# A list schedule for attention: score pairs two at a time on four banks, transfers costed by their bytes, the first batch's loads and small product moved

## The chip, the core and the metric

The kernel runs on one core of a Trainium2 chip: TensorE (PE, matrix products into eight PSUM banks), VectorE (DVE), ScalarE (ACT), GpSimd (POOL) and SyncE (SP), whose queue issues nearly all transfers here. The metric is the time on the device in microseconds, from launch to the last result; lower is better.

## The reference

Talking-heads attention over 4 batches, 12 heads, 448 positions and 64 channels, then a mixture of experts and a two-layer MLP over the 1792 tokens. The change touches attention alone:

```python
def _attn_ref(q, k, v, w_pre, w_post) -> np.ndarray:
    scale = 1.0 / np.sqrt(q.shape[-1])
    scores = scale * np.matmul(q, k.transpose(0, 1, 3, 2))
    scores = np.einsum('bhij,hg->bgij', scores, w_pre)
    scores = scores - np.max(scores, axis=-1, keepdims=True)
    attn = np.exp(scores)
    attn = attn / (np.sum(attn, axis=-1, keepdims=True) + 1e-09)
    attn = np.einsum('bhij,hg->bgij', attn, w_post)
    return np.matmul(attn, v).astype(np.float32)
```

`w_pre` and `w_post` mix the 12 heads before and after the softmax.

## The kernel before, in words

A batch's 448 query rows are cut into chunks of 120, 120, 120 and 88 rows, 16 chunks X in all, and each chunk into blocks n of ten (or fewer) rows times 12 heads, 180 blocks in all. The work on one chunk:

- **Scores** `s`: K and Q come in as `kn`, `qn`, two heads at a time, are transposed on TensorE (`tp`) and split into a high part (`KH`, `QH`, ScalarE) and a low part (`KL`, `QL`, VectorE). A score pair (`qk`) is six row-tiled matmuls for two heads, into two banks; ScalarE or VectorE copies each bank into `S` (line 557).
- **Relay** `x`: a transfer on SyncE's queue gathers the rows of a block from `S`, heads and rows together on the partitions. Six buffers.
- **Pre-mix** `m`: a full matmul with `kpre`; then the maximum (VectorE), the exponential `E` (ScalarE), three small steps on VectorE up to `kr`, the post-mix weights scaled by the sums.
- **Post-mix** `pa`: four matmuls per block into one bank, copied to `AT`. Blocks are post-mixed in order.
- **Products** `px` with V (column-tiled), then `pt`, the small logits products `pl`, `plt`, `pq`.

Besides runs a side job in 64 pieces: load `W`, one step on ScalarE, three on VectorE, store to `wi` or `wo`.

Chunk 0 of the first batch is written out by hand: K and Q come as `fk` and `fq` in pieces, GpSimd copies them together (`beside`), TensorE transposes and multiplies pair after pair; `repeat` is the small product `wps` that spreads `w_pre` and `w_post` (loaded through GpSimd's queue); `spin` is idle work, matmuls of a constant into a bank that nobody reads. All after that is put in order by `Plan`, a list scheduler that runs when the program is built. Each piece of work is a generator that yields steps with the engines it may run on and (time that the engine is held, time until the result), the buffers it takes (`take`) and gives back, and events. The scheduler takes the step that can start first, ties by rank, with a penalty for a change of TensorE's tiling (`TURN`, `LOYAL`), and the instructions of every engine, SyncE's too, stand in the order in which it took them. It decides nothing on the chip: there each engine works down its queue and waits where a semaphore tells it to. Tiles of the eight banks come from `Banks`, in the plan the bank that the plan gave. SyncE's transfers share eight semaphores in turn, so that each waits for the landing of the eighth before it.

Of the kernel before, what the change touches and what calls it, by code (L numbers as in the profile page):

```python
# [48 lines left out]
class Banks:  # L49


    def __init__(self, pool, n):
        self.pool, self.given, self.turns = pool, [], itertools.cycle(range(n))

    def tile(self, shape, dt, tag, name):
        i = self.given.pop(0) if self.given else next(self.turns)
        return self.pool.tile(shape, dt, tag=f"{tag}{i}", name=name)


class Plan:  # L60
# [8 lines left out]
    HOP, TURN, STAY, LOYAL, DRIFT = 0.06, 0.19, 0.02, 2.0, 0.0  # L69

    def __init__(self, slots, banks=None, seed=0):
        self.free = {t: [(0.0, i) for i in range(n)] for t, n in slots.items()}
        self.at, self.engine, self.pending, self.held = {}, {}, [], {}
        self.now = self.reached = 0.0
# [30 lines left out]
    def run(self):  # L105
        while self.pending:
# [36 lines left out]
            end = start + lat  # L143
            for a in step.get("give", ()):
                tag, key = (a, id(task)) if isinstance(a, str) else a
                s = self.held[tag, key if tag == "q" else 0].pop(0)
                self.free[tag] = sorted(self.free[tag] + [(end, s)])
# [4 lines left out]
        if self.banks:  # L152
            self.banks.given = []
            self.banks.turns = itertools.cycle([s for t, s in self.free["q"]])
# [19 lines left out]
def attention(ctx, qctx, tc, q, k, v, w_pre, w_post, wg, xs, lg, ident, nb=4, side=None, route=None):  # L174
# [72 lines left out]
    for h0, h1 in ((0, 2), (2, 4), (4, 8), (8, H)):  # L247
# [210 lines left out]
    with tc.manual_schedule(engines=START):  # L458
        spin(9)
        for j in range(H // 2 + 1):  # L460
            if j < H // 2:
# [6 lines left out]
                if j == 1:  # L468
                    repeat()
                if j > 0:  # L470
                    ps = qk(0, j - 1)
                split_k(0, j, pk)
# [30 lines left out]
    def dma(d):  # L503
        return {"SP": (0.8, d)}
# [3 lines left out]
    def block(n):  # L508
        X, be, rs, m, M = geom(n)
        yield dict(run=dma(4.2), take=["x"], on=[("S", X, h) for h in range(H)], ends=[("x", n)])  # L510
# [32 lines left out]
    def score(X, j):  # L543
# [6 lines left out]
        for i in (j, j + 1):  # L550
            yield dict(run=pe(0.61), tiling="row", onward=True, take=[("q", ("s", X, i, h)) for h in range(2)], on=on, ends=[("s", X, i)])
# [7 lines left out]
    def heads(b, j, s_):  # L559

        tag, src, t = (("kn", k, KN), ("qn", q, QN))[s_]
        yield dict(run=dma(4.0), take=[tag])
# [12 lines left out]
    def values(b):  # L575
        for g in range(4):
            yield dict(run=dma(3.5), on=[("av", 4 * b - 1, 0), ("av", 4 * b - 1, 1)] if b else [("x", 3)], ends=[("V", b)] if g == 3 else [])
# [60 lines left out]
    def piece(i, load, square, bits, store):  # L638
        yield dict(run=dma(6.0), take=["W"])
# [6 lines left out]
        yield dict(run=dma(3.5), give=["W", "sq"])  # L646
# [3 lines left out]
    for h in range(H):  # L650
        plan.at["S", 0, h] = 0.0
    for j in range(H // 2):
        plan.at["K", 0, j] = plan.at["Q", 0, j] = 0.0
    plan.add(4, values(0))
    plan.engine.update(ACT=1.0, DVE=1.0, PE=0.5, SP=0.0)
    for n in range(N):
        plan.add(n, block(n))
    for X in range(1, len(chunks)):
        n0, nb0 = first_of[X], CH[chunks[X - 1][1]][2]
        for j in range(H // 2):  # L660
            r = n0 - 4 - 8 * (X % 4 == 3) - (H - 2 - 2 * j) * (nb0 - 5) / H
# [1112 lines left out]
```

## Time and profile before

| | |
|---|---|
| three timed runs | 1328.36, 1329.72 (median), 1333.59 us |
| the profiled execution | 1326.42 us, span 1324.7 us, granted clock 0.998 |
| TensorE busy | 1300.1 us (98%), 8855 matmuls |
| VectorE, ScalarE busy | 1042.6 us (79%), 824.0 us (62%) |
| attention | 0 to some 500 us |
| experts, MLP | some 530 to 843.6 us, 843.6 to 1324.7 us |

A busy TensorE is not one at its peak: matmuls overlap, and their ends are modelled. Idle time is what stands between the end of one group and the start of the next, and the profile names what ended it.

### The profile page before, as it was taken

How to read it: one execution, taken by the hardware profiler on the slowest of the kernel's cores; microseconds unless marked ns; L12 is line 12 of the kernel's file. 1: busy time of each engine (PE TensorE's matmuls, PEld its weight loads, DVE VectorE, ACT ScalarE, POOL GpSimd, SP SyncE). 2: the span in 40 equal slices, each digit the busy share in tenths (PEclk: the TensorE clock that was granted, in tenths of full speed). 3: DMA queues.
4: the chain of work that ended last, by engine and by line, in shares of the span. 5: the costliest groups of instructions: out<-in, count | busy, mean ns of one | idle time of the engine just before them, and what ended most of it. 6: DMA issues, size and time to landing. Idle time of an engine off the chain costs nothing.

```text
span 1324.7 us, 24862 instructions
## 1 busy us (share of the span) xinstructions
PE 1300.1 (98%) x8855; PEld 1083.7 (82%) x8855; DVE 1042.6 (79%) x2410; ACT 824.0 (62%) x1509; POOL 67.8 (5%) x84
## 2 busy tenths in 40 slices
PE   8899999999999998999999999999999999999997
PEld 5677777677777777899999999998888888888886
DVE  7687888788778889899999999897666666666663
ACT  6566666566666657888889888765444444444432
POOL 3000000000000000100010000011000000001001
PEclk9999999999999999999999999999999999999999
DMA  6758757675757547278545772464433343224201
GB/s 162 229 192 228 228 169 223 203 235 172 218 188 220 175 153 247 87 270 319 185 167 190 286 266 93 147 225 168 152 101 115 108 132 109 85 96 142 94 25 48
DMA packets 146368, 227.02 MB, mean 171 GB/s; under 512 B 44800, under 2 KB 108480, under 8 KB 146240
## 3 DMA queue, kind: packets, MB, share of 16 engines
q1 hardware_dynamic: 139904, 200.20, 46.9%
q0 software_dynamic: 3744, 18.09, 4.0%
q10 hardware_dynamic: 2592, 7.08, 1.4%
q8 instruction: 73, 1.20, 0.4%
q14 instruction: 55, 0.45, 0.1%
HBM read 217.87 MB, written 31.85 MB: 189 GB/s over the span
## 4 chain that ended last, share of the span: by engine, by line
PE 59%; DVE 0%; ACT 0%; POOLq 0%; issue 0%
PE op L1466 18%; PE dh L1522 17%; PE yp L1280 11%; PE h L1246 11%; PE ph L1267 1%; PE px L1174 1%; PE dpt L1403 1%; POOLq L1769 0%; ACT dhs L1526 0%; ACT r L1489 0%; PE gspg L1023 0%; DVE r L1486 0%; DVE r L1487 0%; DVE o L1474 0%; PE pc L1059 0%
## 5 line engine op out<-in xcount | busy, mean ns | idle before, releaser
L1086 DVE TENSOR_TENSOR wl<-r,wh 128x768 fp32r<-128x768 f32 (+1 forms) x246 | 249.1, 1061 | 11.2 <-ACT wh L1085 8.3
L1085 ACT CAST wh<-r 128x768 fp32r<-128x768 f32 (+1 forms) x246 | 224.2, 931 | 37.9 <-PE h L1246 31.1
L536 PEld LDWEIGHTS pa<-kr,E 120*112 120x112 f32 (+1 forms) x1440 | 166.5, 177 | 45.6 <-issue 31.4
L536 PE MATMUL pa<-kr,E 120*112 120x120 f32 (+1 forms) x1440 | 180.7, 269 | 0.8 <-DVE kr L530 0.4
L1086 DVE TENSOR_TENSOR wil<-wi,wih 128x768 fp32r<-128x768 f32 x64 | 60.9, 953 | 131.3 <-ACT wih L1085 131.3
L515 PE MATMUL m<-x,kpre 120*120 120x448 f32 x360 | 159.8, 548 | 3.9 <-DMA x<-S 3.8
L522 ACT ACTIVATE E<-m,nm 120x448 f32<-120x448 f32 x180 | 114.5, 636 | 57.9 <-DVE nm L518 31.5
L1085 ACT CAST wih<-wi 128x768 fp32r<-128x768 f32 x64 | 53.9, 844 | 155.0 <-PE dh L1522 154.0
L518 DVE TENSOR_REDUCE nm<-m 120x1 f32<-120x448 f32 x180 | 111.2, 619 | 26.5 <-PE m L515 22.0
L1466 PE MATMUL op<-woh,gl 128*128 128x512 f32 x448 | 116.8, 341 | 0.0
L1466 PE MATMUL op<-woh,gh 128*128 128x512 f32 x448 | 116.0, 339 | 0.0
L1466 PE MATMUL op<-wol,gh 128*128 128x512 f32 x448 | 115.3, 338 | 0.0
L1522 PE MATMUL dh<-dxh,wih 128*128 128x512 f32 (+1 forms) x384 | 111.2, 364 | 0.1
L1522 PE MATMUL dh<-dxl,wih 128*128 128x512 f32 (+1 forms) x384 | 110.7, 363 | 0.0
L1522 PE MATMUL dh<-dxh,wil 128*128 128x512 f32 (+1 forms) x384 | 109.9, 363 | 0.0
L539 ACT COPY AT<-pa 112x480 f32<-112x480 f32 (+1 forms) x111 | 63.1, 568 | 43.8 <-PE pa L536 41.3
L1085 ACT CAST woh<-wo 128x768 fp32r<-128x768 f32 x64 | 53.4, 836 | 55.2 <-PE op L1466 54.6
L347 PEld LDWEIGHTS px<-AT,vn 112*64 112x64 f32 x1536 | 73.7, 137 | 10.2 <-issue 4.6
L1466 PEld LDWEIGHTS op<-woh,gh 128*128 128x128 f32 x448 | 70.7, 189 | 11.1 <-DVE o L1474 0.3
L1522 PEld LDWEIGHTS dh<-dxl,wih 128*128 128x128 f32 x384 | 70.1, 189 | 11.5
L1522 PEld LDWEIGHTS dh<-dxh,wil 128*128 128x128 f32 x384 | 69.8, 189 | 11.3
L515 PEld LDWEIGHTS m<-x,kpre 120*120 120x120 f32 x360 | 55.1, 183 | 28.9 <-issue 18.2
(290 smaller groups left out, 2561.1 us busy)
## 6 DMA issues: line engine op xcount, KB each, us to landing
r<-in_moe_w_dram SPq DMA_DIRECT2D x54, 1024.0 KB
r<-in_moe_w_dram SPq DMA_DIRECT2D x72, 768.0 KB
x<-S SPq DMA_DIRECT2D x172, 210.0 KB
wi<-wi SPq DMA_DIRECT2D x32, 768.0 KB
wo<-wo SPq DMA_DIRECT2D x32, 768.0 KB
W<-in_moe_w_in_dram SPq DMA_DIRECT2D x32, 384.0 KB
W<-in_moe_w_out_dram SPq DMA_DIRECT2D x32, 384.0 KB
ys<-y ACTq DMA_DIRECT2D x17, 384.0 KB
```

The source lines that it names most:

```text
L347: nc.tensor.matmul(px[64 * e : 64 * e + 64, pr, :n], VN[b, g // 3][:, g % 3, cc], AT[X][:, cc, g, :n], start=(cc == 0), stop=(cc == 3))
L515: nc.tensor.matmul(ps[:M, :S], kpre[:M, :M], x[:M], start=True, stop=True)
L518: nc.vector.reduce_max(nm[:M], ps[:M, :S], axis=AX.X, negate=True)
L522: last["act"] = nc.scalar.activation(e[:M], ps[:M, :S], AF.Exp, bias=nm[:M], scale=1.0, accum_out=sg[:M])
L536: nc.tensor.matmul(pa[:112, c, :120], e[:M, c * 112 : c * 112 + 112], kr[:M], start=True, stop=True)
L539: last["post"] = by[eng](AT[X][:, :, :, j0 : j0 + m], pa[:112, :, :120].rearrange("p c (g i) -> p c g i", i=10)[:, :, :, :m])
L1085: self.latest["A"] = nc.scalar.copy(hi, src).ins
L1086: self.latest["V"] = nc.vector.tensor_tensor(lo, src, hi.bitcast(F32), op=ALU.subtract).ins
L1246: self.nc.tensor.matmul(hp[n], a[:, k], w[:, n * 512 : n * 512 + 512], start=(k == 0 and i == 0), stop=(k == 5 and i == 2))
L1280: self.nc.tensor.matmul(yp[n][:, :384], a[:, k], w[:, n * 384 : n * 384 + 384], start=(k == 0 and i == 0), stop=(k == 7 and i == 2))
L1466: nc.tensor.matmul(bank[:, to], g[:, t * P : t * P + P], w[:, of], start=first, stop=(f == 15 and i == 2), skip_group_check=(n == 1))
L1522: nc.tensor.matmul(hp[:, :N], w[:, k], x[:, k, :N], start=(k == 0 and i == 0), stop=(k == 5 and i == 2))
```

## The change

Five edits. `Plan` gets a model of transfers: SyncE is held for its issue time, and all transfers share one wire that moves `kb` at `RATE` KB/us after `LEAD`, and land `LAND` later; before, each had a fixed time to landing and held SyncE 0.8 us. A score step covers two pairs with four banks in one step, where before each pair was a step and others could come between; the penalty for a change of tiling goes from 2 to 3 ranks, and scores have ranks 2 blocks earlier. `Banks` gives the least recently used bank, the plan starts from the banks' order at the end of the first batch, and its starting times of events and engines are changed. The four-head pieces of K and Q of the first batch are cut in two for heads 4 to 7 (so that two more transfers stand on SyncE's queue). And `wps` moves from the second to the fifth pair, with two `spin` matmuls after the first pair's scores.

```diff
-        self.pool, self.given, self.turns = pool, [], itertools.cycle(range(n))
+        self.pool, self.given, self.turns = pool, [], list(range(n))
...
-        i = self.given.pop(0) if self.given else next(self.turns)
+        i = self.given.pop(0) if self.given else self.turns[0]
+        if i in self.turns:
+            self.turns.remove(i)
+            self.turns.append(i)
...
-    HOP, TURN, STAY, LOYAL, DRIFT = 0.06, 0.19, 0.02, 2.0, 0.0
+    LEAD, LAND, RATE = 0.6, 1.97, 260.0
+    HOP, TURN, STAY, LOYAL, DRIFT = 0.06, 0.19, 0.02, 3, 0.0
...
             end = start + lat
+            if "kb" in step:
+                self.wire = max(self.wire, start + hold + self.LEAD) + step["kb"] / self.RATE
+                end = self.wire + self.LAND
...
-    for h0, h1 in ((0, 2), (2, 4), (4, 8), (8, H)):
+    for h0, h1 in ((0, 2), (2, 4), (4, 6), (6, 8), (8, H)):
         load_first(fk, k, h0, h1)
         load_first(fq, q, h0, h1, slice(0, 2))
...
-                if j == 1:
+                if j == 4:
                     repeat()
                 if j > 0:
                     ps = qk(0, j - 1)
+                if j == 1:
+                    spin(2)
...
-        return {"SP": (0.8, d)}
+        return {"SP": (d, d)}
...
-        yield dict(run=dma(4.2), take=["x"], on=[("S", X, h) for h in range(H)], ends=[("x", n)])
+        yield dict(run=dma(0.86), kb=18 * M // 10, take=["x"], on=[("S", X, h) for h in range(H)], ends=[("x", n)])
...
-        for i in (j, j + 1):
-            yield dict(run=pe(0.61), tiling="row", onward=True, take=[("q", ("s", X, i, h)) for h in range(2)], on=on, ends=[("s", X, i)])
+        js = range(j, j + 2)
+        yield dict(run=pe(0.6 * len(js) + 0.01), tiling="row", take=[("q", ("s", X, i, h)) for i in js for h in range(2)], on=on, ends=[("s", X, i) for i in js])
+        for i in js:
             SC[X, i] = qk(X, i)
...
-        yield dict(run=dma(4.0), take=[tag])
+        yield dict(run=dma(1.36), kb=230, take=[tag])
...
-            r = n0 - 4 - 8 * (X % 4 == 3) - (H - 2 - 2 * j) * (nb0 - 5) / H
+            r = n0 - 6 - 8 * (X % 4 == 3) - (H - 2 - 2 * j) * (nb0 - 5) / H
```

Loads of V and of the pieces and stores of the pieces get issue times and bytes in the same way.

What the order of instructions becomes at three places. First TensorE in the first batch, from the second pair's transposes (`tp0_1`) to the third's (`tp0_2`); `s0_0` and `s0_1` are the first score pair. Before:

```order
L216 MATMUL tp0_1_1_0_263<-ident_64,qn0_1_256 128x112 x2
L437 MATMUL wps_266<-wpp_205,rep_210 120x24
L284 MATMUL s0_0_270<-KH0_0_246,QH0_0_250 120x448
L284 MATMUL s0_1_271<-KH0_0_246,QH0_0_250 120x448
L284 MATMUL s0_0_270<-KL0_0_247,QH0_0_250 120x448
L284 MATMUL s0_1_271<-KL0_0_247,QH0_0_250 120x448
L284 MATMUL s0_0_270<-KH0_0_246,QL0_0_251 120x448
L284 MATMUL s0_1_271<-KH0_0_246,QL0_0_251 120x448
L216 MATMUL tp0_2_0_0_292<-ident_64,kn0_2_288 128x112 x4
L216 MATMUL tp0_2_1_0_297<-ident_64,qn0_2_290 128x112 x2
```

and now:

```order
L222 MATMUL tp0_1_1_0_265<-ident_64,qn0_1_258 128x112 x2
L290 MATMUL s0_0_269<-KH0_0_248,QH0_0_252 120x448
L290 MATMUL s0_1_270<-KH0_0_248,QH0_0_252 120x448
L290 MATMUL s0_0_269<-KL0_0_249,QH0_0_252 120x448
L290 MATMUL s0_1_270<-KL0_0_249,QH0_0_252 120x448
L290 MATMUL s0_0_269<-KH0_0_248,QL0_0_253 120x448
L290 MATMUL s0_1_270<-KH0_0_248,QL0_0_253 120x448
L462 LDWEIGHTS ones_107
L462 MATMUL spin2_277<-ones_107 128x512
L462 LDWEIGHTS ones_107
L462 MATMUL spin2_277<-ones_107 128x512
L222 MATMUL tp0_2_0_0_294<-ident_64,kn0_2_290 128x112 x4
```

The small product `wps` is gone from between transposes and scores, and two `spin` matmuls stand behind the scores.

Second, SyncE's queue from block 6's relay to block 12's (`vn0_1`, `vn0_2` are the second and third piece of V of batch 0, `W1` a piece of the side job, `wi` a store of it, `qn1_1` Q of batch 1). Before:

```order
L301 DMA x6_593<-S0_269 120x1x448
L301 DMA x7_606<-S0_269 120x1x448
L301 DMA x8_620<-S0_269 120x1x448
L203 DMA vn0_1_629<-in_v_dram 112x3x256
L301 DMA x9_645<-S0_269 120x1x448
L301 DMA x10_653<-S0_269 120x1x448
L301 DMA x11_663<-S0_269 120x1x448
L194 DMA qn1_1_675<-in_q_dram 112x4x64 x2
L203 DMA vn0_2_685<-in_v_dram 112x3x256
L1579 DMA W1_693<-in_moe2_w_in_dram 128x768
L301 DMA x12_703<-S1_468 120x1x448
```

and now:

```order
L307 DMA x6_591<-S0_268 120x1x448
L307 DMA x7_609<-S0_268 120x1x448
L307 DMA x8_618<-S0_268 120x1x448
L307 DMA x9_634<-S0_268 120x1x448
L307 DMA x10_644<-S0_268 120x1x448
L209 DMA vn0_1_658<-in_v_dram 112x3x256
L307 DMA x11_663<-S0_268 120x1x448
L200 DMA qn1_1_676<-in_q_dram 112x4x64 x2
L1590 DMA W1_691<-in_moe2_w_in_dram 128x768
L1606 DMA wi_62<-f0_675 128x384
L307 DMA x12_703<-S1_476 120x1x448
```

The second V piece stands behind `x10` and no longer behind `x8`, the third is gone from this stretch, and a store stands before `x12`.

Third, the transposes of batch 1. TensorE from behind the fifth pair's transposes (`tp1_4`) to the sixth's of K (`tp1_5_0`), with the first score pair of chunk 4 among them, before:

```order
L536 MATMUL pa34_1732<-kr34_1720,E34_1647 112x120 x4
L515 MATMUL m39_1748<-x39_1634,kpre_202 120x448
L284 MATMUL s4_0_1760<-KH1_0_1431,QH1_0_1505 120x448
L284 MATMUL s4_1_1761<-KH1_0_1431,QH1_0_1505 120x448
L284 MATMUL s4_0_1760<-KL1_0_1432,QH1_0_1505 120x448
L284 MATMUL s4_1_1761<-KL1_0_1432,QH1_0_1505 120x448
L284 MATMUL s4_0_1760<-KH1_0_1431,QL1_0_1506 120x448
L284 MATMUL s4_1_1761<-KH1_0_1431,QL1_0_1506 120x448
L536 MATMUL pa35_1774<-kr35_1757,E35_1696 112x120 x4
L216 MATMUL tp1_5_0_0_1795<-ident_64,kn1_5_1717 128x112 x4
```

and now from just ahead of that transpose:

```order
L544 MATMUL pa33_1718<-kr33_1701,E33_1654 112x120 x4
L523 MATMUL m37_1729<-x37_1608,kpre_204 120x448
L222 MATMUL tp1_5_0_0_1736<-ident_64,kn1_5_1661 128x112 x4
L544 MATMUL pa34_1752<-kr34_1741,E34_1671 112x120 x4
L523 MATMUL m38_1762<-x38_1643,kpre_204 120x448
L290 MATMUL s4_0_1772<-KH1_0_1358,QH1_0_1378 120x448
L290 MATMUL s4_1_1773<-KH1_0_1358,QH1_0_1378 120x448
L290 MATMUL s4_0_1772<-KL1_0_1359,QH1_0_1378 120x448
L290 MATMUL s4_1_1773<-KL1_0_1359,QH1_0_1378 120x448
L290 MATMUL s4_0_1772<-KH1_0_1358,QL1_0_1379 120x448
L290 MATMUL s4_1_1773<-KH1_0_1358,QL1_0_1379 120x448
L290 MATMUL s4_2_1780<-KH1_1_1408,QH1_1_1531 120x448
```

The transpose of `kn1_5` now stands ahead of the first score pair, and the second pair (`s4_2`, `s4_3`) follows the first at once. The loads for it on SyncE's queue, before:

```order
L194 DMA kn1_4_1651<-in_k_dram 112x4x64 x2
L194 DMA qn1_4_1665<-in_q_dram 112x4x64 x2
L1579 DMA W11_1678<-in_moe2_w_in_dram 128x768
L301 DMA x40_1688<-S3_1102 120x1x448
L301 DMA x41_1699<-S3_1102 120x1x448
L1595 DMA wi_62<-f10_1661 128x384
L194 DMA kn1_5_1717<-in_k_dram 112x4x64 x2
L194 DMA qn1_5_1737<-in_q_dram 112x4x64 x2
```

and now:

```order
L200 DMA kn1_4_1581<-in_k_dram 112x4x64 x2
L307 DMA x37_1608<-S3_1076 120x1x448
L200 DMA qn1_4_1620<-in_q_dram 112x4x64 x2
L1606 DMA wi_62<-f9_1571 128x384
L307 DMA x38_1643<-S3_1076 120x1x448
L200 DMA kn1_5_1661<-in_k_dram 112x4x64 x2
L307 DMA x39_1685<-S3_1076 120x1x448
L307 DMA x40_1699<-S3_1076 120x1x448
```

Two relays, `x40` and `x41`, a piece and its store stood between the loads of `qn1_4` and `kn1_5`; now one store and `x38` do, while `x37` has come in between `kn1_4` and `qn1_4`.

## Rows read from the trace of the kernel before

**Rows 1.** Windows by stage: length, busy PE PEld DVE ACT POOL (instructions), granted clock, DMA share, GB/s.

```profile
0.00:61.60 61.60, 53.56 (x395) 36.03 (x395) 41.81 (x145) 34.26 (x82) 10.59 (x36) 0.97 0.74 204
61.60:497.00 435.40, 430.51 (x3934) 328.91 (x3933) 354.63 (x1202) 276.97 (x674) 1.23 (x2) 1.00 0.65 199
...
532.40:843.60 311.20, 311.18 (x1720) 285.12 (x1721) 293.56 (x377) 272.23 (x363) 23.16 (x21) 1.00 0.57 203
```

**Rows 2.** Waits of TensorE from 0 to 532 us: total us, times, longest.

```profile
PE m L515 <- DMA x<-S: 3.8, 6, 2.0
PE tp L216 <- DMA kn<-in_k_dram: 3.6, 4, 1.2
...
PE tp L216 <- ACT KH L571: 0.6, 1, 0.6
```

**Rows 3.** Busy time in two windows of the start, columns as in rows 1.

```profile
11.20:14.60 3.40, 3.40 (x18) 2.03 (x14) 2.37 (x5) 1.99 (x5) 2.44 (x6) 0.50 1.01 179
...
40.00:60.00 20.00, 18.34 (x159) 13.05 (x161) 13.43 (x46) 11.44 (x29) 0.00 (x0) 1.00 0.86 260
```

**Rows 4.** Timeline of TensorE, first batch: start, us, instruction, count, [idle before <- releaser].

```profile
6.07 0.61 PE L456 MATMUL spin<-ones 128*128 128x512 bf16 x2
...
9.04 0.35 PE L437 MATMUL wps<-wpp,rep 12*120 12x24 f32 x2 [1.12 <-DMA wpp<-in_w_post_dram]
...
11.96 1.01 PE L216 MATMUL tp<-ident,kn 112*128 112x112 f32 x4
...
16.20 0.60 PE L216 MATMUL tp<-ident,kn 112*128 112x112 f32 x4
...
21.79 0.47 PE L284 MATMUL s<-KH,QH 64*120 64x448 f32 x2 [1.48 <-DVE QL L235]
```

**Rows 5.** Timeline of GpSimd, copies of K and Q of the first batch.

```profile
8.63 0.61 POOL L254 COPY kn<-fk 112x512 f32<-112x512 f32 x1 [1.03 <-DMA fk<-in_k_dram]
9.74 0.40 POOL L254 COPY qn<-fq 112x256 f32<-112x256 f32 x1 [0.50 <-DMA fq<-in_q_dram]
...
12.62 0.40 POOL L254 COPY qn<-fq 112x256 f32<-112x256 f32 x1 [0.31 <-DMA fq<-in_q_dram]
```

**Rows 6.** Timelines of SyncE's queue and TensorE, the first relays.

```profile
19.78 5.63 SPq L301 DMA_DIRECT2D x<-S  x6
25.53 1.47 SPq L194 DMA_DIRECT2D kn<-in_k_dram  x2
...
41.61 0.98 PE L515 MATMUL m<-x,kpre 120*120 120x448 f32 x2 [0.36 <-DMA x<-S]
```

**Rows 7.** Timelines of TensorE and SyncE's queue, transposes of batch 1.

```profile
106.29 0.55 PE L216 MATMUL tp<-ident,kn 112*128 112x112 f32 x4
...
113.61 1.66 SPq L194 DMA_DIRECT2D kn<-in_k_dram  x2
...
118.38 0.58 PE L216 MATMUL tp<-ident,kn 112*128 112x112 f32 x4 [1.17 <-DMA kn<-in_k_dram]
```

**Rows 8.** Timeline of TensorE, around two places with score pairs.

```profile
44.00 0.98 PE L536 MATMUL pa<-kr,E 120*112 120x120 f32 x8
44.91 0.46 PE L284 MATMUL s<-KH,QH 64*120 64x448 f32 x2
...
45.71 1.07 PE L536 MATMUL pa<-kr,E 120*112 120x120 f32 x8
...
120.97 0.47 PE L284 MATMUL s<-KH,QH 64*120 64x448 f32 x2
...
121.68 0.36 PE L284 MATMUL s<-KH,QH 64*120 64x448 f32 x2
```

**Rows 9.** Line 557 on ScalarE, the copies of scores.

```profile
L557 ACT COPY S<-s x118: 515/534/570, 22.7 to 449.1; 120x448 f32<-120x448 f32 x86, 88x448 f32<-88x448 f32 x32
```

**Rows 10.** Timeline of all engines, the last block of attention.

```profile
496.28 0.92 PE L515 MATMUL m<-x,kpre 108*108 108x448 f32 x2
...
499.40 0.28 DVE L530 TENSOR_SCALAR kr<-kpost,rs 108x120 f32<-108x120 f32 x1
```

More of the change, by code (lines that the diff above doesn't have):

```diff
@@ L73, in __init__ @@
         self.at, self.engine, self.pending, self.held = {}, {}, [], {}
-        self.now = self.reached = 0.0
+        self.now = self.reached = self.wire = 0.0
         self.tiling, self.banks, self.luck = "full", banks, random.Random(seed)
@@ L152, in run @@
         if self.banks:
-            self.banks.given = []
-            self.banks.turns = itertools.cycle([s for t, s in self.free["q"]])
+            self.banks.given, self.banks.turns = [], [s for t, s in self.free["q"]]
 class Taken:
@@ L576, in values @@
         for g in range(4):
-            yield dict(run=dma(3.5), on=[("av", 4 * b - 1, 0), ("av", 4 * b - 1, 1)] if b else [("x", 3)], ends=[("V", b)] if g == 3 else [])
+            yield dict(run=dma(0.58), kb=344, on=[("av", 4 * b - 1, 0), ("av", 4 * b - 1, 1)] if b else [("x", 3)], ends=[("V", b)] if g == 3 else [])
             load_v(b, g)
@@ L638, in piece @@
     def piece(i, load, square, bits, store):
-        yield dict(run=dma(6.0), take=["W"])
+        yield dict(run=dma(0.58), kb=393, take=["W"])
         load(i)
@@ L645, in piece @@
             op()
-        yield dict(run=dma(3.5), give=["W", "sq"])
+        yield dict(run=dma(0.42), kb=197, give=["W", "sq"])
         store(i)
@@ L650, in attention @@
     for h in range(H):
-        plan.at["S", 0, h] = 0.0
+        plan.at["S", 0, h] = 0.7
     for j in range(H // 2):
-        plan.at["K", 0, j] = plan.at["Q", 0, j] = 0.0
+        plan.at["K", 0, j] = 0.0
+        plan.at["Q", 0, j] = 1.4 + 0.4 * j
+    plan.free["q"] = [(max(0.0, 0.6 + 0.4 * (i - 1)) if i > 1 else 0.0, s) for i, s in enumerate(pq.turns)]
     plan.add(4, values(0))
-    plan.engine.update(ACT=1.0, DVE=1.0, PE=0.5, SP=0.0)
+    plan.engine.update(ACT=3.0, DVE=3.3, PE=2.2, SP=0.0)
     for n in range(N):
```

## The prediction

> **What bounds the kernel now.** I read the busy time by stage first, then the waits of TensorE in the attention stage, then the timeline at each wait, and last the order of the instructions on TensorE and SyncE. The stages [rows 1] show where this change can act at all. The experts (532.4 to 843.6 us) and most of the rest keep TensorE busy without a gap, and the diff doesn't touch them. It touches the first 497 us, attention. There TensorE is busy 53.56 of the first 61.6 us and 430.51 of the next 435.4, so 8.0 and 4.9 us are idle: this is a kernel bound by TensorE, and what can be won is the idle time, the time at half clock and the price of switching between row-tiled and full matmuls. VectorE, at 354.63 of 435.4 us, is no bound.
>
> The waits [rows 2] split into two families. One is the start: 3.8 us in six waits of the pre-mix `m` for its relayed tile `x`, besides 1.12 us before the product `wps` and 1.48 for the low part of Q before chunk 1's scores [rows 4]. The other is the change of batch: 3.6 us in four waits of a transpose for `kn`, and 0.6 us for the bank after one of them. The granted clock adds a third loss: it stood at 0.50 (1.2 GHz) from 11.2 to 14.6 us [rows 3], after TensorE had idled before `wps`. Four transposes that take 0.60 us at the full level took 1.01 us there [rows 4].
>
> The sum is made against the profiled execution, 1326.42 us (span 1324.7 and 1.7 outside it). The three timed runs have their median at 1329.72 us, 3.3 us above it; I carry the difference of the sum over to the median.
>
> **The start, step by step.** (a) `wps` waited 1.12 us for w_post, with everything on TensorE behind it: the engine had been free since 7.9 us, and the first score pair, whose inputs were ready, came only after `wps` [rows 4]. In the new order that pair goes at once and `wps` stands three pairs later. Next come transposes of the third pair, whose K and Q go through copies on GpSimd that waited for transfers until 8.63, 9.74 and 12.62 us [rows 5]. Between 8.63 and 12.62 landed 229 + 459 + 229 KB (four heads of half Q, four heads of K, four heads of half Q), 230 KB/us. With the four-head pieces halved, K of heads 4 and 5 is there 229 KB, 1.0 us, sooner, at 7.6, and with Q's half after it and the two copies (0.61 and 0.40) the transposes can start near 8.7 instead of 10.12. The last piece, though, still ends at 12.62, since the bytes are the same; copies of the last pair end near 14.05, and its transposes, now at 16.20 [rows 4], can't be earlier than that. I take 14.7: 1.5 us won. The half clock is inside this: 3.4 us at 1.01 to 0.60 are 1.4 us lost, and with a gap less and two more `spin` matmuls behind the first pair it need not fall again. The earlier two took 0.61 us [rows 4]; these lie in the wait for the third pair's K, and would cost that much without it.
>
> (b) Of 33 tiles that went round the eight banks the last, a late transpose, is in bank 0; the plan gave chunk 1's first scores banks 0 and 1, and so they waited 1.48 us for the last of six low parts [rows 4]. With banks by least recent use they start on the bank of the last score pair. That win is not a separate one: behind these scores `m` waits for `x` anyway.
>
> (c) Relays. Before `x6` to `x10` SyncE now issues no second V piece, before `x12` to `x16` no third and fourth, and the third weight piece moved too (the order below shows the first). A V piece is 344 KB, so at 230 KB/us each is 1.5 us. Against this the first K load of batch 1 now stands ahead of `x0`; its two issues took 1.47 us, before the six relays' 5.63 they now come first [rows 6]. That uses up the 1.5 us of (a) for `x0`, which has time behind chunk 1's scores, but not for `x6`, which has the same work ahead of it as before. `m10`, at 41.61 after a wait [rows 6], should so come some 3 us earlier, and by `m16` up to 4.5.
>
> Of 1.1 + 1.5 + 3.8 us of waits and 1.4 us of clock, 7.8 in all, I take 4.3 back. The lower bound is 0 (the bytes set `x`, below), the upper 7.8.
>
> **The change of batch.** `kn1_5` could be loaded when the transpose of `kn1_3` had read its slot, near 106.8 us, but SyncE came to it at 113.61, and its transpose waited 1.17 us until 118.38 [rows 7]: 4.8 us from issue to use. In between SyncE had issued other things, two relays that themselves waited for slots among them. In the new order only `x37`, `qn1_4`, one store and `x38` stand between `kn1_4` and `kn1_5`. With 0.94 us for a relay (5.63 / 6), 1.5 for a pair of loads [rows 6] and half a microsecond for a store, `kn1_5` issues an estimated 2.2 us after the transpose of `kn1_3` has read its slot and is there at 7.0. Work on TensorE from that transpose to its own is six `m`, three `pa` and three transposes, 8.1 us: slack of 1.1. For batch 3 the same count gives 2 us and more. So of 3.6 + 0.6 us I take 3.8 back; bounds 0.5 (thin slack lost to a backlog) and 4.2.
>
> **The switches.** A post-mix `pa` of 0.82 us takes 0.91 (44.00 to 44.91) when scores follow, and a score pair 0.80 (44.91 to 45.71) when `pa` follows, against 0.71 (120.97 to 121.68) when a second pair follows [rows 8]: 0.18 us for going in and out. The order has 54 unbroken runs of score pairs before and 47 now, 41 of them of two pairs. Seven times 0.18 is 1.3 us; bounds 0, if pairs in a run wait for banks, and 2.7, at 0.18 for each of the 15 changes of tiling of every kind that the order has less (129, was 144).
>
> **What is added.** Four banks at once leave four for everything else. In the trace no score pair waits for a copy after chunk 1's first [rows 2], and a copy out of a bank takes 0.53 us on ScalarE [rows 9]. The Trainium skill's page TensorEngine Tiling (Array Packing), section Restrictions and Gotchas (PSUM pressure), speaks against the edit: row tiles write to different banks, and tiling raises the pressure on them. By that rule each four-bank step would tend to wait for a copy; what it would cost is the third rival. By the rows two or three such waits are enough for the sum: 1.0 us. The end of attention gets worse: from the start of `m179` to the scaled weights of its block pass 3.4 us (496.28 to 499.40, and 0.28 for the last step) [rows 10], and the new order has `m179`, `pa177`, `pa178` and small products there, 2.4 us; 1.0 us of wait, some 0.5 more than now. Together 1.5 us lost; bounds 0 and, by the rival, 22.
>
> **Sum.** 4.3 + 3.8 + 1.3 - 1.5 = 7.9 us: the profile at 1318.5, the median at 1321.8, 0.6% faster. No stage behind attention should give it back: its transfers are issued behind attention's own, and it starts when attention ends.
>
> **Rivals.**
> 1. The start gives nothing, since its bytes set `x` and not their order. For it: the DMA engines' share is 0.86 from 40 to 60 us [rows 3]. Against it: V is needed only at the first `px`, which both orders put behind `m16`. Then 7.9 - 4.3 = 3.6 won: 1326.1.
> 2. The change doesn't do what it says: the new transfer costs move the waits to other places but don't shorten them, and the switches won are eaten by the end of attention. For it: slack at `kn1_5` is about 1 us. Then 1329.7.
> 3. Four banks. If each of the 42 four-bank steps in the runs waits for one copy of 0.53 us, 22 us are lost and the time is 1344. The win is gone from 15 such waits on (7.9 / 0.53), and the kernel is over 0.5% slower from 28 on. For it: the page's rule. Against it: by the order as much work on TensorE stands between two uses of a bank as before.
> 4. All comes back: 7.8 + 4.2 + 2.7 - 0.5 = 14.2, so 1315.5. For it: every gap has its own cause that the order removes.
>
> **How the numbers follow.** My forecast has 0.60, rivals 1 to 4 have 0.15, 0.12, 0.06 and 0.07. The forecast's own range, half of the start and half of the switches either way, is 1317 to 1326; I put 0.47 of its 0.60 below 1323.07, the time at which it is 0.5% faster, which is about what a measurement here can tell from no change. Faster: 0.47 + 0.07 = 0.54. Same: 0.13 + 0.15 + 0.12 = 0.40. Slower: 0.06. The range that leaves out 2 in 10 goes from 1315 (little beyond rival 4) to 1328.5: out of it fall rival 3, most of rival 2 and a tail below.
>
> **What the new profile would show.** Right: no half clock after 5 us; `wps` without a wait; `m10` near 38.5 us and the first `px` some 4 us earlier; transposes of `kn` waiting less than 1 us in all; attention's last `pa` about 8 us earlier; the experts' and the last stage's lengths unchanged. Wrong: waits of `m` for `x` still near 4 us (rival 1), waits of scores for copies (rival 3), or new waits of `pa` for `kr` beyond the last block, which I priced at nothing since the order has more work between `m` and `pa` than before.

## The result, and the profile after

| | changed | before |
|---|---|---|
| timed runs | 1317.87 us median (1315.67 to 1319.75, 6 runs) | 1329.53 us median (1328.36 to 1333.85, 6 runs) |
| profiled execution | 1317.96 us, span 1316.0 | 1326.42 us, span 1324.7 |
| first `h` matmul, behind attention | 496.48 us | 505.97 us |

The ratio is 0.9911, 95% interval 0.9893 to 0.9928: 0.9% faster. Between the profiled executions 8.5 us were won, between the medians 11.7: the profiled execution before was quicker than each of the six timed runs, the one after lies at their median. The first `h` (the first matmul of the experts) came 9.5 us earlier. Of that 0.8 us were lost again by the start of the third window below, where the prediction had priced nothing.

By stage, over windows of the changed kernel that answer to [rows 1] (the second ends 9 us earlier, the third starts 8.7 earlier), columns as there:

```profile
0.00:61.60 61.60, 56.50 (x409) 37.90 (x411) 44.91 (x150) 35.54 (x85) 10.53 (x36) 0.97 0.77 205
61.60:488.00 426.40, 424.09 (x3933) 328.42 (x3929) 355.99 (x1210) 271.21 (x663) 1.31 (x2) 1.00 0.67 203
523.70:834.90 311.20, 309.33 (x1711) 282.97 (x1710) 293.43 (x377) 272.16 (x362) 21.07 (x20) 1.00 0.57 202
```

TensorE's idle time fell from 8.0 to 5.1 us in the first stage and from 4.9 to 2.3 in the second. The granted clock of the first stage is 0.97 as before. The waits of TensorE from 0 to 532 us answer to [rows 2] (total us, times, longest):

```profile
PE m L523 <- DMA x<-S: 3.3, 4, 2.1
PE tp L222 <- DMA qn<-in_q_dram: 1.8, 1, 1.8
...
PE tp L222 <- POOL kn L260: 0.6, 1, 0.6
```

No transpose waits for `kn` from memory, and no score waits at all. But `m` still waits 3.3 us for `x`, nearly as long as before. The timeline of TensorE at the start (start, us, instruction, count, [idle before <- releaser]) answers to [rows 4] and to the last of [rows 6]:

```profile
8.38 0.61 PE L462 MATMUL spin<-ones 128*128 128x512 bf16 x2
...
12.46 0.60 PE L222 MATMUL tp<-ident,kn 112*128 112x112 f32 x4 [0.57 <-POOL kn L260]
...
13.55 0.38 PE L443 MATMUL wps<-wpp,rep 12*120 12x24 f32 x2
...
14.66 0.60 PE L222 MATMUL tp<-ident,kn 112*128 112x112 f32 x4
...
18.54 0.47 PE L290 MATMUL s<-KH,QH 64*120 64x448 f32 x2
...
24.49 6.57 PE L523 MATMUL m<-x,kpre 120*120 120x448 f32 x12 [2.08 <-DMA x<-S]
...
41.97 0.98 PE L523 MATMUL m<-x,kpre 120*120 120x448 f32 x2 [0.78 <-DMA x<-S]
...
57.18 1.04 PE L353 MATMUL px<-AT,vn 112*64 112x120 f32 x16
```

`wps` waits for nothing, the last pair's transposes start at 14.66 (16.20 before, 14.7 forecast), and chunk 1's scores at 18.54 (21.79 before). So 3.25 us were in hand there against this one execution of before. Then the first `m` waits 2.08 us, and starts 1.1 us earlier than before (24.49 for 25.59). SyncE's queue shows why (to be read with [rows 6]), and the granted clock behind the wait (TensorE busy, clock, DMA share, GB/s) what it brought with it:

```profile
18.50 1.42 SPq L200 DMA_DIRECT2D kn<-in_k_dram  x2
20.03 5.13 SPq L307 DMA_DIRECT2D x<-S  x6
```

```profile
25.70:29.20 3.50, 3.50 (x6) 0.51 0.79 205
29.20:33.00 3.80, 3.80 (x26) 1.00 0.88 272
```

`x0` is issued at 20.03, behind the K load, where before it was issued at 19.78. The half clock (1.2 GHz), which stood at 11.2 to 14.6 us before [rows 3], stands at 25.7 to 29.2 now: between these two executions it was moved, not removed. That need not hold of every execution: this one had a mean granted clock of 0.997, five of the six timed runs of the same kernel had 0.999, so they spent less time at half clock.

At the change of batch the steps that answer to [rows 7] are these, TensorE and SyncE's queue:

```profile
101.36 0.55 PE L222 MATMUL tp<-ident,kn 112*128 112x112 f32 x4
...
105.19 1.26 SPq L200 DMA_DIRECT2D kn<-in_k_dram  x2
...
110.11 0.57 PE L222 MATMUL tp<-ident,kn 112*128 112x112 f32 x4
...
225.27 0.58 PE L222 MATMUL tp<-ident,qn 112*128 112x112 f32 x4 [1.82 <-DMA qn<-in_q_dram]
```

From the end of the transpose that frees the slot (101.9) to the load pass 3.3 us (6.8 before, 2.2 forecast), and the pair's own transpose comes 8.75 us after the first (8.1 forecast) without a wait. One new wait of 1.82 us stands in batch 2, for a Q pair. The last block, which answers to [rows 10], on VectorE and TensorE:

```profile
490.56 0.28 DVE L538 TENSOR_SCALAR kr<-kpost,rs 108x120 f32<-108x120 f32 x1
...
490.98 1.05 PE L544 MATMUL pa<-kr,E 108*112 108x120 f32 x8 [0.25 <-DVE l L175]
```

### The profile page after: what moved, and what is told of

Same layout as the page of the kernel before. It is cut to its first block, busy times and chain, and to the rows that moved or that the text cites. A ratio compares the mean times of both kernels' runs of the same rounds, so it can differ in the third digit from the quotient of the medians.

```text
span 1316.0 us, 24862 instructions
## 1 busy us (share of the span) xinstructions
PE 1296.0 (98%) x8857; PEld 1084.1 (82%) x8857; DVE 1046.5 (80%) x2419; ACT 818.8 (62%) x1500; POOL 65.9 (5%) x84
## 4 chain that ended last, share of the span: by engine, by line
PE 59%; DVE 0%; ACT 0%; issue 0%; POOLq 0%; ACTq 0%
PE op L1477 18%; PE dh L1533 17%; PE yp L1291 11%; PE h L1257 10%; PE ph L1278 1%; PE px L1185 1%; PE dpt L1414 1%; ACT wh L1096 0%; DVE wl L1097 0%; POOLq L1780 0%; ACT dhs L1537 0%; ACT r L1500 0%; DVE xl L1195 0%; PE gspg L1034 0%; DVE r L1498 0%
## 5 line engine op out<-in xcount | busy, mean ns | idle before, releaser
L547 ACT COPY AT<-pa 112x480 f32<-112x480 f32 (+1 forms) x105 | 59.6, 568 | 46.2 <-PE pa L544 42.6
L1533 PEld LDWEIGHTS dh<-dxh,wih 128*128 128x128 f32 x384 | 68.4, 189 | 11.6 <-ACT dhs L1537 0.3
```

Source lines behind the costliest of these rows:

```text
L547: last["post"] = by[eng](AT[X][:, :, :, j0 : j0 + m], pa[:112, :, :120].rearrange("p c (g i) -> p c g i", i=10)[:, :, :, :m])
L1533: nc.tensor.matmul(hp[:, :N], w[:, k], x[:, k, :N], start=(k == 0 and i == 0), stop=(k == 5 and i == 2))
```

## The experiments

I name the parts **S** (first batch and banks), **T** (transfers costed by their bytes), **P** (two score pairs in one step) and **R** (the two smaller edits of the plan: `LOYAL` from 2 to 3, and scores with ranks two blocks earlier). R was not run by itself. It is in the changed kernel and in every kernel made from it by taking a part out, and not in those made from the kernel before by putting a part in, so a comparison across the two groups has R in it. Each expectation below was written before its run. The theory from the trace was that the parts add: S some 3 us, T 2.7, P 2.4. The expectations go by the last post-mix product `pa179` (500.0 us before, 491.0 changed), the readings also by the first `h`. The rivals were that four banks cost something, and that any new order of such a plan moves the time by some microseconds.

**S alone.** The kernel before with these edits and the plan's due times:

```diff
-    for h0, h1 in ((0, 2), (2, 4), (4, 8), (8, H)):
+    for h0, h1 in ((0, 2), (2, 4), (4, 6), (6, 8), (8, H)):
-                if j == 1:
+                if j == 4:
                     repeat()
+                if j == 1:
+                    spin(2)
```

> The kernel before with the edits of the first batch and of the banks alone (smaller pieces, wps three pairs later, two spins, least recent use of banks, the plan's due times for the first copies); scores one pair at a time and transfers at the old costs. The measure beside the time is the start of the last post-mix product pa179: 500.03 us before, 490.98 with all edits. Parts add up: the start won 3.0 us in the trace of the changed kernel, so pa179 at 497.0 and the waits of transposes for kn still near 3.6 us. Only together: a schedule made by a plan is shifted by every edit, and the part alone gives anything from 496 to 502. The start gives nothing: pa179 within 0.5 of 500.0.

Measured: 1327.6 us median (10 runs), ratio 1.0002 (0.9984 to 1.0020). In its profiled execution `pa179` starts at 505.8 us, outside all three branches, and the first `h` at 511.7, 5.7 us later than before; that execution lay 4.9 us above the median of its runs. Waits of TensorE from 0 to 480 us:

```profile
PE m L519 <- DMA x<-S: 5.2, 3, 3.5
PE tp L218 <- DMA kn<-in_k_dram: 2.0, 3, 1.3
PE tp L218 <- DMA qn<-in_q_dram: 1.8, 4, 0.5
```

The banks and pieces do what the order says, and `m` waits longer for `x` (5.2 us, 3.8 before). From 60 us on most of what it loses against before lies at one place, three waits of transposes (0.74, 0.64 and 0.55 us) and 6.8 us at half clock behind them:

```profile
241.01 0.57 PE L218 MATMUL tp<-ident,qn 112*128 112x112 f32 x4 [0.74 <-ACT AT L543]
...
243.34 0.98 PE L218 MATMUL tp<-ident,qn 112*128 112x112 f32 x4 [0.55 <-DMA qn<-in_q_dram]
...
245.66 7.26 PE L349 MATMUL px<-AT,vn 112*64 112x120 f32 x96
```

```profile
243.20:250.00 6.80, 6.66 (x54) 5.80 (x56) 3.46 (x11) 2.75 (x7) 0.00 (x0) 0.50 0.84 209
```

The same 96 matmuls of `px` take 5.14 us in the kernel before (at 55.74). By the time of its runs the part alone is worth nothing.

**T alone.** The kernel before with this and the same for the other four kinds of transfer:

```diff
+            if "kb" in step:
+                self.wire = max(self.wire, start + hold + self.LEAD) + step["kb"] / self.RATE
+                end = self.wire + self.LAND
-        return {"SP": (0.8, d)}
+        return {"SP": (d, d)}
-        yield dict(run=dma(4.0), take=[tag])
+        yield dict(run=dma(1.36), kb=230, take=[tag])
```

> The kernel before with transfers costed by their bytes alone. Parts add up: the waits of transposes for kn and for the bank behind them (4.2 us before) go, and one new wait of the kind seen after the change (1.8 us) may stand: pa179 at 497.2 to 496.0 (500.03 before), with the start unchanged to 25 us. Costs only move waits (the second rival): pa179 within 0.7 of 500.0, the kn waits gone and others of the same length in their place.

Measured: 1317.59 us (1316.6 to 1319.56, 4 runs), ratio 0.9920 (0.9897 to 0.9943): nearly the whole gain from this part. The first `h` is at 499.3, 6.7 of the 9.5 us, and `pa179` 6.3 us earlier than before, beyond the 2.8 to 4.0 expected. Waits from 0 to 480 us:

```profile
PE m L519 <- DMA x<-S: 2.5, 4, 0.9
PE s L288 <- DVE QL L239: 1.5, 1, 1.5
...
PE tp L220 <- DMA qn<-in_q_dram: 1.0, 1, 1.0
```

The four waits for `kn` are gone (rival 2 falls), and the waits for `x` at the start are shorter too, though the start's code is that of before.

**P alone.**

```diff
-        for i in (j, j + 1):
-            yield dict(run=pe(0.61), tiling="row", onward=True, take=[("q", ("s", X, i, h)) for h in range(2)], ...)
+        js = range(j, j + 2)
+        yield dict(run=pe(0.6 * len(js) + 0.01), tiling="row", take=[("q", ("s", X, i, h)) for i in js for h in range(2)], ...)
```

> The kernel before with two score pairs in one step alone, so four banks taken at once. Parts add up: eight changes of tiling and seven runs of scores fewer at about 0.18 us a run, and by the trace of the changed kernel some more: 1.3 to 2.5 us, pa179 at 498.7 to 497.5, no wait of scores for a copy beyond chunk 1's first. Four banks cost (the third rival): waits of s for ScalarE's or VectorE's copies near 0.53 us each, many of them, pa179 later than 500.5.

Measured: 1327.9 us (10 runs), ratio 1.0002 (0.9991 to 1.0013). The waits from 30 to 480 us hold none of a score, so rival 3 falls (though `pa179`, at 500.57 us, just meets its bound of 500.5):

```profile
PE m L515 <- DMA x<-S: 5.8, 4, 2.7
PE tp L216 <- DMA kn<-in_k_dram: 2.0, 2, 1.1
...
PE tp L216 <- ACT S L558: 0.5, 1, 0.5
```

But four banks at once are not quite free: a transpose now waits 0.5 us for a copy of scores (`S`), an `m` 0.2 for another, and in the kernel without T (below) a transpose 1.0, waits that the kernel before doesn't have. The changes of tiling were saved, but not much was won by it. I took each step's time from its start to the next's, less the quickest time of its kind (`m` 0.751, `pa` 0.820, a score pair 0.606, a transpose 0.383 us). From 60 to 480 us, going from scores to full matmuls costs 6.4 us in 42 places before and 3.8 in 38 here. But from one score pair to the next 3.8 us in 42 places, against 2.2 in 36. With the waits all this stretch loses 28.9 us against 29.8, and the first 60 lose 0.6 more.

**P undone** (the changed kernel with the pair's old step, so S, T and R).

> The changed kernel with scores one pair at a time again. Parts add up: 136 changes of tiling instead of 126 and 54 runs of scores instead of 47, so pa179 1.3 to 2.5 us later than the 490.98 of the changed kernel, 492.3 to 493.5. Four banks cost: pa179 earlier than 490.5. Only together: the plan without pairs puts a K load elsewhere as well (it stands after two relays instead of ahead of them), and a difference beyond 3 us either way comes from waits for transfers and not from tiling.

Measured: 1314.78 us (1313.94 to 1317.23, 4 runs), ratio 0.9899 (0.9877 to 0.9922). The first `h` is at 497.0, 0.5 us later than with P, and `pa179` 0.6 us later, where 1.3 to 2.5 were expected. By the trace P is worth a little beside S, T and R, by the time nothing.

**S undone** (T, P and R) and **T undone** (S, P and R).

> The changed kernel without the edits of the first batch and of the banks: transfer costs and pairs together. If pairs are worth nothing or a little less than nothing beside the transfer costs (two at once stood 2.2 us above one at a time with the K load moved in both): a ratio of 0.991 to 0.994. If the pairs are worth the 1.3 us of the prediction: 0.991 or less, and faster than the start edits with the transfer costs, 0.9899.

> The changed kernel with the old costs of transfers: the edits of the start and the pairs together. If the transfer costs carry the change, as the runs of each part alone say (start 1.0002 and pairs 1.0002 of the time before, transfers 0.992): a ratio of 0.997 to 1.002. If parts pay only together: 0.992 to 0.996.

Measured without S: 1313.18 us (1312.72 to 1315.84, 4 runs), ratio 0.9881 (0.9862 to 0.9899), the first `h` at 491.2, 5.3 us ahead of the changed kernel. This is the fastest of all, under the 0.991 that the expectation set for pairs that are worth something, and the edits of the start are what it leaves out. Without T: 1322.44 us (1318.14 to 1328.25, 4 runs), ratio 0.9935 (0.9913 to 0.9957). I had expected 0.997 or more, or 0.992 to 0.996 if parts pay only together: the number is in the latter range. But S, P and R are worth 0.65% together here, while S and P alone are worth nothing, so either parts pay only together or R carries it. No run tells the two apart. The timeline of TensorE without S, the first relays:

```profile
24.22 4.77 PE L519 MATMUL m<-x,kpre 120*120 120x448 f32 x12
34.13 4.11 PE L519 MATMUL m<-x,kpre 120*120 120x448 f32 x10
39.72 0.98 PE L519 MATMUL m<-x,kpre 120*120 120x448 f32 x2 [0.35 <-DMA x<-S]
```

TensorE comes to the first `m` 1.8 us later than it does with S (24.22 against 24.49 less the wait of 2.08), finds its `x` there, keeps its clock, and starts `m6` to `m10` 2 us earlier (34.13 against 36.20). Of these 2 us 1.8 are the half clock: `m0` to `m5` take 4.77 us here and 6.57 in the profiled execution with S.

**The two halves of T**, each in the kernel before: SyncE held for as long as a transfer's issues take, with the old landing times; and landing by bytes, with SyncE held 0.8 us by each.

```diff
 # the first
-        return {"SP": (0.8, d)}
+        return {"SP": d}
-        yield dict(run=dma(4.0), take=[tag])
+        yield dict(run=dma((1.36, 4.0)), take=[tag])
 # the second
-        yield dict(run=dma(4.0), take=[tag])
+        yield dict(run=dma(4.0), kb=230, take=[tag])
```

> The kernel before with one half of the transfers' costs: SyncE is held by each transfer as long as its issues take (0.42 to 1.36 us instead of 0.8 for all), while the landing times stay the old constants (3.5 to 6.0 us). If the gain of the transfer costs alone (10 us of time, last pa from 500.0 to 493.7) comes from a right count of SyncE's own time, most of it is here: last pa before 496.5, waits for kn under 1.5 us. If it comes from the bytes on the wire: last pa within 1.5 us of 500, waits of transposes for kn near 3.6 us.

> The other half: the landing of each transfer by its bytes at 260 KB/us behind the transfers ahead of it, while SyncE is held 0.8 us by each as before. If the bytes are what counts: last pa before 496.5 and waits for kn under 1.5 us. If SyncE's time is what counts: last pa within 1.5 us of 500. By its order it has 60 runs of scores against 54, six more, at 0.1 to 0.18 us each up to 1 us against it in either case.

Measured: 1323.08 us, ratio 0.9945 (0.9927 to 0.9962), and 1324.56 us, ratio 0.9971 (0.9953 to 0.9989). The first half holds some two thirds of it, the second one third (0.55% and 0.29%, T 0.80%; the intervals of the two overlap a little). By the trace they are nearer: `pa179` starts at 496.0 and 496.9 us, 4.0 and 3.1 us earlier than before, where T alone gives 6.3. So the first meets the condition set for it (before 496.5, waits for `kn` under 1.5 us), the second only that on the waits. Both shorten the waits of transposes, from 60 to 480 us, the first half and then the second:

```profile
PE tp L216 <- DMA qn<-in_q_dram: 1.6, 3, 0.7
PE tp L216 <- DMA kn<-in_k_dram: 0.8, 2, 0.6
```

```profile
...
PE tp L220 <- DMA kn<-in_k_dram: 0.5, 1, 0.5
```

**The K load behind the relays.** In the changed kernel, and in the one without P, batch 1's first K pair is issued behind `x5`; nothing else changes its place on any engine.

```diff
-        load_pair(b, j, ...)
+        if (b, j, s_) != (1, 0, 0):
+            load_pair(b, j, ...)
         relay(n)
+        if n == 5:
+            load_pair(1, 0, ..., k, KN)
```

> The changed kernel with one load moved on SyncE: batch 1's first K pair is issued behind the six relays x0 to x5 instead of ahead of them; no other engine's order differs. If that load is what m0 waits for (the step of the prediction that gave it 1.5 us of slack was wrong): x0 issues 1.4 us earlier, near 18.6, m0's wait falls from 2.08 to about 0.6 us, the half clock behind it (3.4 us, 1.7 lost) may stay away, and the last pa comes 1.4 to 3.1 us earlier than the 490.98 of the changed kernel. If the transfers' bytes set x and not their order: m0 within 0.4 us of 24.5, or the same idle a few m later, and the last pa within 0.5 us of 491.

> Scores one pair at a time (the fastest kernel so far) and batch 1's first K load behind x0 to x5, on SyncE alone. If the load is what m0 waits for: x0 issues near 17.7 instead of 19.16, m0's wait falls from 2.44 to about 1.0 us, and the last pa comes 1 to 1.5 us earlier than with single pairs alone. If bytes set x: the same waits within 0.4 us. Single pairs no worse than two at once: the ratio to the kernel before again at or under 0.990.

Measured: 1317.21 us (1316.93 to 1317.9, 4 runs), ratio 0.9898 (0.9862 to 0.9933), and without P 1314.97 us (1312.91 to 1316.32, 4 runs), ratio 0.9882 (0.9845 to 0.9920). The first `h` is at 497.3, where 1.4 to 3.1 us earlier than 496.5 was expected, and at 493.7 without P, 3.3 us earlier than 497.0, where 1 to 1.5 was expected. By the time neither differs clearly from its kernel without the move (1317.87 and 1314.78 us). The timeline of TensorE in the first:

```profile
22.24 1.01 PE L525 MATMUL m<-x,kpre 120*120 120x448 f32 x2
23.48 4.66 PE L525 MATMUL m<-x,kpre 120*120 120x448 f32 x10 [0.23 <-DMA x<-S]
33.84 1.89 PE L525 MATMUL m<-x,kpre 120*120 120x448 f32 x4 [0.40 <-DMA x<-S]
...
38.98 0.98 PE L525 MATMUL m<-x,kpre 120*120 120x448 f32 x2 [0.71 <-DMA x<-S]
41.84 0.98 PE L525 MATMUL m<-x,kpre 120*120 120x448 f32 x2 [1.05 <-DMA x<-S]
```

The load did hold up `x0`: issued at 17.98 instead of 20.03, the first `m` runs 2.2 us earlier, and the clock stays at 1.00. But by 41.84 TensorE is where it was (41.97). From 18.5 to 60 us `m` waits 2.9 us in six places, and 3.1 us in three without the move. What was saved at `x0` is waited for at `x6` to `x11`. In the kernel without P, too, one wait of 2.0 us for `x` is left near 39 us. These two ran on one chip and differ in P alone: without it the time is 2.2 us shorter, and the ranges of their runs don't meet, while beside T alone P and R are worth 4.4 us (1317.59 to 1313.18, on two chips).

**Is it luck?** One constant of the plan that has nothing to do with the change, `HOP`, moved in both kernels:

```diff
-    HOP, TURN, STAY, LOYAL, DRIFT = 0.06, ...
+    HOP, TURN, STAY, LOYAL, DRIFT = 0.08, ...
```

> The changed kernel with one constant of the plan that no edit speaks of moved: the hop between engines 0.08 us instead of 0.06. It changes the order a little and has no reason to be better or worse. If the gain is a lucky order: a ratio anywhere from 0.988 to 1.000. If it is from the causes named: within 0.3% of the changed kernel, 0.988 to 0.994.

> The kernel before with the same constant moved, 0.08 instead of 0.06. If before had an unlucky order, and the change is what any new order would give: a ratio under 0.995. If the causes named hold: 0.997 to 1.003, with waits of transposes for kn and qn of 3 us or more, as in before.

Measured: 1318.24 us, ratio 0.9907 (0.9885 to 0.9928), for the changed kernel, and 1329.03 us, ratio 0.9995 (0.9983 to 1.0007), for the one before. By the time a reshuffled order alone moved neither. By the trace it did move the second: its profiled execution has the first `h` at 511.1 us, 5.1 later than before, with half clock from 11.4 to 14.8 and from 38.7 to 42.1 us. It also missed the rest of its expectation: transposes wait 2.5 us for `kn` and `qn`, not 3 or more, and only 0.4 of it for `kn`; 1.5 us for `kr` stand before another transpose. So waits for `kn` can go and others come, with no gain, by an edit that has nothing to do with transfers; with T the time fell too. One constant in two kernels is a small sample, and it doesn't bound the noise of the plan.

The eight kernels with and without S, T and P, with the loss of TensorE in three stretches of the profiled execution (worked out as for P, waits included):

| | ratio | first `h`, us | 0 to 18.5 | 18.5 to 60 | 60 to 480 | profile less median, us | at half clock, 5 to 480 us |
|---|---|---|---|---|---|---|---|
| before | 1 | 506.0 | 5.0 | 8.3 | 29.8 | -3.1 | 3.4 |
| S | 1.0002 | 511.7 | 2.4 | 10.9 | 35.1 | 4.9 | 10.2 |
| P | 1.0002 | 506.5 | 4.8 | 9.1 | 28.9 | 5.7 | 3.4 |
| S, P, R | 0.9935 | 501.4 | 2.9 | 12.0 | 24.0 | 5.8 | 6.8 |
| T | 0.9920 | 499.3 | 4.6 | 6.8 | 25.9 | 2.0 | 0 |
| T, S, R | 0.9899 | 497.0 | 2.1 | 7.0 | 25.1 | 2.5 | 0 |
| T, P, R | 0.9881 | 491.2 | 5.0 | 3.2 | 20.7 | 0.3 | 0 |
| T, S, P, R (changed) | 0.9911 | 496.5 | 2.9 | 7.3 | 23.5 | 0.1 | 3.5 |

The ratio is of several runs; all columns behind it are of one profiled execution each. The last two say how far that execution lay from the median of its kernel's runs, and how long it stood at half clock in attention. A difference of a few us between two rows of the trace can be one of executions and not of kernels.

Each ratio is against runs of before on the same chip. S wins 1.9 to 2.6 us by 18.5 us wherever it is added, but does not keep them to 60: in the next stretch it loses 2.6 us more alone, and 4.1 beside T, P and R, 1.8 of these by the half clock of that one execution. T is worth 0.8% alone and 0.2% beside S, P and R. The rows beside one other part differ in R as well and don't price S or T.

## Why the prediction was right, and which steps failed

**The sum held, its last step did not.** Forecast were 7.9 us against the profiled execution, and 8.5 came. The median came out at 1317.87 where I had said 1321.8, because I carried the 3.3 us by which the runs' median lay above the profile over to the changed kernel. There the profile lies at the median. Of the 3.9 us that the forecast was too slow, 3.3 are this step and 0.6 the sum. Executions of one kernel differ by more than that, and with the granted clock: of 19 runs of before on one chip the three at 0.995 or 0.996 took 1329.6 to 1331.5 us, the four at 0.999 1324.7 to 1328.2. That the sum itself came within 0.6 us is partly luck: by the trace the start and the change of batch gave about a microsecond less than forecast each, the switches about one more, and the new waits cost about one less, as the next paragraphs show. The range was also added wrongly: half of the start and half of the switches are 2.15 and 0.65 us, which make 1319.0 to 1324.6 and not 1317 to 1326, and the measured median lies below that.

**The start, 4.3 us: over-sized.** By the trace the loss to 60 us fell by 3.1 us (5.0 + 8.3 to 2.9 + 7.3). Step (a) met its number, transposes at 14.66 for 14.7, but not by its mechanism. P alone has the start's code of before, and its last pair's transposes stand at the same time:

```profile
8.99 0.35 PE L437 MATMUL wps<-wpp,rep 12*120 12x24 f32 x2 [1.07 <-DMA wpp<-in_w_post_dram]
...
14.66 0.60 PE L216 MATMUL tp<-ident,kn 112*128 112x112 f32 x4
```

So do those of the other kernels with the old start whose clock stayed at 1.00 behind `wps` (T 14.47, the one without S 14.81, the halves of T 14.36 and 14.46), while the one with `HOP` moved, where it fell again, has 16.59. Between the two profiled executions the 1.5 us of (a) are the half clock of the one before. Against kernels with the old start at full clock the new order of `wps` and the smaller pieces gave at most 1.1 us there (13.73 to 14.66 in the table's kernels with S, 14.47 to 14.81 in those without). Step (b) held: the scores go without their wait of 1.48 us. Step (c) failed in the words "for `x0`, which has time behind chunk 1's scores". It had none: with (a) and (b) the scores end 2 us before `x0` is there, and the half clock that "need not fall again" fell behind that wait. The K load was only the first cause, as the run that moves it shows; behind it the same idle time appears at later relays. Which of the transfers in front of those relays hold them up was not taken apart further: in the order that waits least (without S) `x6` is issued at 27.9 us and batch 1's second K pair behind `x11`, in that run `x6` at 28.8 and the pair ahead of it. The sign of rival 1, waits of `m` near 4 us, came (3.3), though not its price: that order and not bytes alone sets `x` is shown by the kernel without S, where they are 0.4 us. `m10` was forecast near 38.5 and came at 39.4. The first `px` was to come 4 us earlier and came 1.4 later, since the order had put more blocks in front of it.

**The change of batch, 3.8 us: the waits were right.** The idle time of TensorE from 60 to 480 us fell by 2.6 us (4.8 to 2.2), with the `kn` waits at nothing and one new wait of 1.82 us. What I had not seen is that T does far more than that. Alone it carries 0.80% of the 0.89% by the time and 6.7 of the 9.5 us at the first `h`, and part of what I booked under the start is T's doing (loss to 60 us 13.3 to 11.4). Each half of the new cost gives a part of it. Part of T's gain in the time is the clock: the median granted clock of the runs is 0.998 or 0.999 in every kernel with T or a half of it, 0.995 to 0.998 in those without, and 0.001 of it is an estimated 1.3 us (of 1320 us, TensorE being busy). Why the clock falls less often with T was not taken apart.

**The switches, 1.3 us: under-sized in the trace, not a win by themselves.** In the stretch from 60 to 480 us they cost 3.9 us less in the changed kernel, with P and R in it (13.7 to 9.9, for 13 changes of tiling fewer), and 1.5 of it went back between the pairs that now follow each other, which leaves 2.4. Alone the part moved no time.

**New waits, -1.5 us: mostly absent.** From 60 to 480 us no score waited for a copy out of a bank in any of the kernels with two pairs in a step. The Trainium skill's page TensorEngine Tiling (Array Packing), section Restrictions and Gotchas, warns that row tiling increases the pressure on banks; the traces show it only at the edge, in the transposes and the `m` above that wait 0.2 to 1.0 us for a copy of scores in P alone and in the kernel without T, and not in the changed kernel. The end of attention has 0.52 us of wait, at the last two `pa`, against 0.28 before; I had priced it at 1.0.

**The parts don't add, and the prediction added them.** T alone is worth 0.80%, S, P and R without T 0.65%, and all together 0.89%: T is enough for nearly the whole gain, but most of it also comes without T. Which of S, P and R carries that 0.65% is not shown. All together are worth less than T, P and R by 0.3% in the time (the intervals overlap a little) and by 5.3 us at the first `h`. Shown is that the kernel without S is not slower than the changed one, and that S's early win beside T, P and R is waited away at `x`, with the half clock behind the wait on top in the profiled execution. That S alone loses most from 60 to 480 us (35.1) is for some 3 of the 5.3 us the half clock near 245 us, and for 1.1 us more waiting (5.9 for 4.8). Why its order has those waits stays open, and with one profiled execution of it so does whether each execution loses its clock there.

## What to carry to other kernels

When a list schedule decides the order, price what it decides with first: costing the transfers by SyncE's hold per transfer and by bytes gave nearly the whole win in time by itself. Work brought forward on the busy engine counts only as far as the next transfer is brought forward too; look at the issue of that transfer before booking the gain. And don't add the gains of parts that share one planner: time the combinations, with every small edit assigned to a part, since here the fastest kernel was one with a part left out. And before a gain is read from two traces, look whether other kernels with the same code at that place show it too: here the gain booked for one step was the half clock of a single execution.

## What was not expected of the hardware

The first gather of the experts on GpSimd (an indirect transfer, `xg`) is of very different length in executions of nearly the same program. In the changed kernel, in the one with `HOP` moved, and in P alone (start, us):

```profile
512.93 1.45 POOL L1177 DMA_INDIRECT xg<-xs,ids  x1 [41.62 <-DMA r<-in_moe_w_dram]
521.55 0.95 POOL L1177 DMA_INDIRECT xg<-xs,ids  x1 [7.17 <-PEq L1693]
```

```profile
512.12 7.73 POOL L1177 DMA_INDIRECT xg<-xs,ids  x1 [37.76 <-DVE ids L962]
```

```profile
522.70 7.73 POOL L1167 DMA_INDIRECT xg<-xs,ids  x1 [37.58 <-DMA r<-in_moe_w_dram]
...
538.87 0.94 POOL L1167 DMA_INDIRECT xg<-xs,ids  x1 [8.44 <-PEq L1683]
```

The second takes 0.94 or 0.95 us in each, the first 1.45, 3.19 (before) or 7.73: in 14 profiled executions five, five and four times. TensorE then waits 0 to 0.4, 1.8 to 2.2 and 6.3 or 6.4 us for it. This has nothing to do with attention, and is in the time: P alone has its first `h` 0.5 us behind that of before, but a span 7.2 us longer. Of the other 6.7 us 4.5 are this wait, and the rest goes with the 6.8 us at half clock behind it (columns as in rows 1):

```profile
531.50:538.30 6.80, 5.12 (x18) 4.87 (x18) 1.12 (x2) 1.44 (x3) 0.00 (x0) 0.50 0.14 50
```

With one profiled execution of each kernel it stays open whether the length goes with the kernel or with the execution. That is why the table gives the first `h`.

Nor does a wait decide alone whether the clock falls. Behind 1.12 us of idle before `wps` it fell to 0.50 in the kernel before, behind 1.3 us at the same place in the kernel without S it stayed at 1.00. Behind the wait of 2.08 us for `x0` it fell to 0.51 in the changed kernel, while with P undone, in TensorE's timeline and the window (columns as in rows 1), it did not:

```profile
23.38 3.63 PE L523 MATMUL m<-x,kpre 120*120 120x448 f32 x8 [2.44 <-DMA x<-S]
```

```profile
23.30:27.00 3.70, 3.62 (x10) 1.21 (x10) 2.22 (x7) 1.58 (x5) 0.00 (x0) 1.00 0.70 227
```
